# Fourier filter and routed experts on one core: the sign copy goes to VectorE, some transfers are cut anew, and the written-out order is planned again

## The chip, the cores and the metric

One core of one Trainium2 chip. The metric is the device time in microseconds (us) of one execution, as a median over runs. TensorE (PE, with its weight loads PEld), VectorE (DVE), ScalarE (ACT), GpSimd (POOL) and the transfers that SyncE (SP) and POOL issue all run side by side; every engine takes its own instructions in the order in which the kernel wrote them.

## The reference

```
X  = rfft(x, axis=1)                      # x: 8 x 2496 x 256, float32
Yr = X.real @ w_r - X.imag @ w_i + b_r
Yi = X.real @ w_i + X.imag @ w_r + b_i
Y  = soft_threshold(Yr, 0.01) + 1j * soft_threshold(Yi, 0.01)
t  = irfft(Y, n=2496, axis=1).reshape(19968, 256)
e  = argmax(t @ w_gate);  g = softmax(t @ w_gate)[e]       # 8 experts
out = g * (relu(t @ w1[e]) @ w2[e])       # w1: 256 x 1024, w2: 1024 x 256 per expert
```

## The kernel before

**Forward part.** The transform of length 2496 = 39 x 64 is two steps of matmuls. For each of 8 batches: x is loaded in six pieces (`load_x`), `s1` does the step of 39 in fp32, its result goes out to DRAM (`s1_store`, tile zd) and comes back turned (`zload`, tile zs) in five pieces of four frequencies. Each piece i then runs through a chain: `s2` (step of 64, fp32, with the constant cd), `s2_hi` on ACT and `s2_lo` on DVE split the result into two f16 halves in tile xa, `s2_neg` writes the negative of one third of xa into another third (line 542, on POOL), `wmul` multiplies by the complex weight (48 matmuls, lines 554 to 556, the last 24 of which read the negated part), `thr`, `thr_pos`, `thr_sub`, `thr_out`, `thr_lo` are the threshold and a second split (DVE, ACT, DVE, ACT, POOL line 586), `inv1` (lines 600 and 602, constant ce; line 602 reads what `thr_lo` wrote) is the first step back, and `vstore` puts it to DRAM (vd).

**Back part.** For each batch `vload`, `inv2`, a split, a transpose, the logits, the routing on DVE, and 22 scatters by POOL (line 770) that put token rows into the list of their expert. Batches 0 and 1 go back early, the others during the expert phase. `vzero` writes zeros behind each batch's part of vd, `fillers` writes 256 rows of no token ahead of each expert's list, from a tile that takes the only buffer "cl", which `thr_pos` needs for every piece.

**Expert weights.** 16 matrices are loaded (`wprep_load`), measured, split into f16 halves (ACT, and DVE line 818) and stored. The first expert block waits for the tables of batches 0 and 1 and for all 16.

**Expert part.** 92 blocks (71 of 256 rows, 21 of 128): `fetch_x`, `fetch_w`, `up` (lines 983 to 985), relu and split (lines 989, 994, 999), `down` (lines 1010 to 1012), a gate on ACT and a scatter to the output by POOL (line 1021).

**Order.** `Plan` places all this. Every piece of work is a task with an engine, a cost, predecessors, buffers and a rank; when an engine is idle the plan takes the ready task of lowest rank whose buffers are free. A transfer of rank above 0 is held while the planned transfer backlog exceeds BACK; one of rank 0 or less is not held. ORDER adds to the rank by kind of task, MARGIN adds a delay after the last predecessor, BEGIN replaces a task's earliest time, INV0 and INVD set when batches from 2 on may go back, WT0 and WTD when the matrices may be loaded (matrix u from WT0 + WTD x u). The plan only writes the order of instructions on each engine; on the chip each waits for its semaphores.

```
ld = A("SP", 1.0, wprep_load, u, take=[wa], dma=3.25, rank=0.5, after=WT0 + WTD * u)
n_ = A("POOL", 1.6, s2_neg, b, i, deps=[l], rank=0, early=1.5)
if t["dma"] and t["rank"] > 0 and dq - now > BACK:
```

Of the kernel before, what the change touches and what calls it, by code (L numbers as in the profile page):

```python
# [22 lines left out]
SLOTS = 22  # L23
K1 = 20
# [104 lines left out]
BUF = {"bt": 2, "zt": 2, "zs": 2, "xa": 2, "u": 2, "cl": 1, "sh": 1, "vt": 2, "vs": 2, "yt": 2, "yr": 6}  # L129
EPOCHS = {2:12,3:22,4:31,5:41,6:51,7:61}  # L130
JS, NPRE = 12, 2
SCD = 2.6
INV0, INVD, WT0, WTD = 355, 85, 135, 9
ORDER = {"fetch_x": -19, "inv1": 37, "inv1_hi": -7, "inv1_lo": -22, "inv2:p": -261, "inv2_hi:p": -3, "inv2_lo:p": -42,
    "load_x": 53, "load_x:0": 42, "logits:p": -73, "norm_part": 60, "route3:p": 44, "route_hot:p": 45,
    "s1": -48, "s1_store": 22, "s2_lo": -39, "s2_neg": -60, "scatter:p": -3, "table": 29, "thr_lo": -26,
    "thr_pos": 29, "thr_sq": 17, "vstore": 12, "w_lo": -14, "wmul": 70, "wprep_hi": 27, "wprep_lo": 27,
    "wprep_scale": 16, "wprep_sq": 30, "wprep_store": 33, "xscale": 9, "ynorm:p": 148, "yscale:l": 40,
    "ytrans:p": 45}
MARGIN = {"inv2:l": 3, "inv2:p": 5, "logits:l": 1, "logits:p": 11, "norm_sum": 6, "route2:l": 0, "route2:p": 7,  # L140
    "s2": 2, "wprep_sum": 3, "ynorm:l": 5}
BEGIN = {"fillers": 81, "load_b": 15, "load_cd": 28, "load_ce": 47, "load_g": 23, "load_rest": 70, "load_w": 5,
    "vzero": 52}
ZD = 3
KS = 4

# [21 lines left out]
class Plan:  # L168


    LAT, DLAT, BACK = 0.2, 2.0, 3

    def __init__(self, bufs):
        self.t, self.bufs, self.mark = [], bufs, {}
# [101 lines left out]
def build(ctx: ExitStack, tc: tile.TileContext, x, w_r, w_i, b_r, b_i, wg, w1, w2,  # L276
          c_c, c_cg, c_d, c_e, c_tri, c_32, c_blk, out):
    nc = tc.nc
    B = x.shape[0]
    V, S, P, T, Q = nc.vector, nc.scalar, nc.gpsimd, nc.tensor, nc.sync  # L280
# [4 lines left out]
    dram = ctx.enter_context(tc.tile_pool(name="dram", bufs=1, space=bass.MemoryType.DRAM))  # L285
# [17 lines left out]
    fpool = fw.enter_context(tc.tile_pool(name="fp", bufs=2))  # L303
# [25 lines left out]
    cd = fcst.tile([128, K1, 128], F32, name="cd")  # L329
    ce = fcst.tile([128, K1, 2, 128], F16, name="ce")  # L330
# [13 lines left out]
        for q in range(4):  # L344
            Q.dma_start(wgs[32 * q:32 * q + 32], wg.rearrange("(b i o) e -> i b o e", i=32, o=2))

    def load_cd():
        Q.dma_start(cd, c_d.rearrange("p (k m) -> p k m", k=K1))

    def load_ce():  # L350
        Q.dma_start(ce, c_e.rearrange("p (k h m) -> p k h m", k=K1, h=2))

    def load_rest():
        Q.dma_start(c32, c_32)
# [7 lines left out]
    zero = fpool.tile([128, 1024], F16, name="vt", bufs=BUF["vt"])  # L362
    V.memset(zero, 0.0)

    zd = [dram.tile([K1, 66, 2, D], F32, name=f"zd{i}") for i in range(ZD)]
    vd = [dram.tile([K1, 66, 2, 512], F16, name=f"vd{i}") for i in range(B)]

    def vzero():
        for i in range(B):
            Q.dma_start(vd[i][:, 64:66].rearrange("k n r c -> k n (r c)"), bc(zero[:K1, :], 2))  # L370


    sc = cst.tile([128, 16], F32, name="sc")
# [165 lines left out]
    def s2_neg(b, i):  # L539
        xa = st[b][("xa", i)]  # L540
        xf = xa.rearrange("p j h c -> p (j h) c")
        P.tensor_scalar(xf[:, :, 0:64], xf[:, :, 128:192], -1.0, None, op0=ALU.mult)  # L542

    def wmul(b, i):

# [278 lines left out]

    def fillers():

        fr = fpool.tile([128, RC], F16, name="cl", bufs=BUF["cl"])
        V.memset(fr, 0.0)
        V.memset(fr[:, 512:514].bitcast(I32), 1 << 24)
        fu = fr.bitcast(U16)  # L830
        rv = rows.rearrange("(e r) c -> e r c", e=NE)
        for e in range(NE):
            Q.dma_start(rv[e, 0:256, 0:RC].rearrange("(h p) c -> p h c", p=128), bc(fu, 2))


    MX = max(n for _, _, n, _ in TABS)
# [182 lines left out]
    def down_store(j, t):  # L1019
# [3 lines left out]
        for k in scat2:  # L1023
# [25 lines left out]
    def ns_(c):  # L1049
        return min(4, SLOTS - 4 * c)  # L1050


    wu, zv, fcl = L.buf("u"), L.buf("vt"), L.buf("cl")
    i_cc = A("SP", 0.5, load_cc, rank=0, dma=0.2)
    ld0 = [A("SP", 1.3, load_x, 0, 4 * c, min(SLOTS, 4 * c + 4), rank=0, dma=2.3 * ns_(c) / 4) for c in range(6)]
    i_w = A("SP", 1.6, load_w, rank=0, dma=1.8, take=[wu])
    i_b = A("SP", 1.2, load_b, rank=0, dma=0.6)
    i_g = A("SP", 1.7, load_g, rank=0, dma=0.5)
    i_cd = A("SP", 0.8, load_cd, rank=0, dma=4.8)
    i_r = A("SP", 1.8, load_rest, rank=0.4, dma=2.0, after=26.0)  # L1060
    i_ce = A("SP", 0.8, load_ce, rank=0.2, dma=4.5, after=25.0)
    i_z = A("SP", 4.0, vzero, rank=0.4, dma=0.5, after=40.0, free=[zv])
    A("PE", 6.9, warm, 16, rank=0, take=[zv], free=[zv])
    p_q = A("ACT", 2.0, wsquare, deps=[i_w, i_b, i_g], rank=1)
    p_s = A("PE", 0.2, wsum, deps=[p_q], rank=-100)
# [3 lines left out]
    wp_ = A("DVE", 1.6, w_lo, deps=[wh_], rank=0.5, free=[wu])  # L1069
    gp_ = A("ACT", 0.8, g_hi, deps=[p_p], rank=0.6)  # L1070
    gp_ = A("DVE", 0.8, g_lo, deps=[gp_], rank=0.6)
    fl = A("SP", 5.0, fillers, rank=5, dma=4.0, after=60.0, take=[fcl], free=[fcl])
    s1l, nps, lastz = {}, {}, {}
    scat_t, rt3, tabs, prevtab = {}, {}, {}, None
    last_tab = {}
# [5 lines left out]
    for u in range(2 * NE):  # L1081
        wa, wb = L.buf(f"wt{u % 2}0"), L.buf(f"wt{u % 2}1")
        ld = A("SP", 1.0, wprep_load, u, take=[wa], dma=3.25, rank=0.5, after=WT0 + WTD * u)
        sq = A("ACT", 2.1, wprep_sq, u, deps=[ld], rank=1.2)
        sm_ = A("PE", 0.2, wprep_sum, u, deps=[sq, wst_.get(("sc", u - 1))], rank=-100)
        scl = wst_["sc", u] = A("DVE", 1.5, wprep_scale, u, deps=[sm_], rank=1, take=[wb])
        for i in range(2):
            h = A("ACT", 0.95, wprep_hi, u, i, deps=[scl], rank=1.2)
            l = A("DVE", 1.2, wprep_lo, u, i, deps=[h], rank=1.2, free=[wa])
            wst_[u, i] = A("SP", 0.5, wprep_store, u, i, deps=[l], dma=1.4, rank=0.5, free=[wb])  # L1090
    wdone = [t for k, t in wst_.items() if k[0] != "sc"]

# [1 line left out]
    for b in range(B):  # L1094
        F = 10 * b

        ld = [] if b else ld0
        for c in range(6):
            if b:
                ld.append(A("SP", 1.3, load_x, b, 4 * c, 4 * c + ns_(c), deps=[s1l[b - 1, c], nps[b - 1][c]],  # L1100
                            rank=0.3, dma=9.2 * ns_(c) / 22))
        nm = A("DVE", 0.1, norm, b, deps=[fin1.get(("xs", b - 1))])
        nps[b] = [A("DVE" if not b and i % 2 else "ACT", 1.05, norm_part, b, i, deps=[nm, ld[i]], rank=1)
# [16 lines left out]
        for i in range(5):  # L1120
            zs_, p2_, xa_, pw_, u_, cl_, sh_, pa_, vt_ = (L.buf(n) for n in ("zs", "mm", "xa", "mm", "u", "cl", "sh", "mm", "vt"))
            zl = A("SP", 0.55, zload, b, i, deps=sts, take=[zs_], free=[zdb], dma=8.8 / 5, rank=0)
            t = A("PE", 1.82, s2, b, i, deps=[zl, i_cd], take=[p2_, xa_], free=[zs_], rank=F + 3)
            h = A("ACT", 1.0, s2_hi, b, i, deps=[t, xs], rank=1)
            l = A("DVE", 1.2, s2_lo, b, i, deps=[h], free=[p2_], rank=1)
            n_ = A("POOL", 1.6, s2_neg, b, i, deps=[l], rank=0, early=1.5)
            w = A("PE", 5.22, wmul, b, i, deps=[n_, wp_], take=[pw_, u_], free=[xa_], rank=F + 2)
            th = A("DVE", 1.15, thr, b, i, deps=[w, xs], free=[pw_, btb], rank=0)
            cl = A("ACT", 1.05, thr_pos, b, i, deps=[th], take=[cl_], rank=0)
            sb_ = A("DVE", 1.21, thr_sub, b, i, deps=[cl], free=[cl_], rank=0)  # L1130
            hi = A("ACT", 0.96, thr_out, b, i, deps=[sb_], take=[sh_], free=[u_], rank=0)
            lo = A("POOL", 2.15, thr_lo, b, i, deps=[hi], free=[u_], rank=0, early=0.8)
            sqs.append(A("ACT", 1.05, thr_sq, b, i, deps=[sb_], free=[u_], rank=0.5))
            v1 = A("PE", 1.32, inv1, b, i, deps=[lo, hi, i_ce], take=[pa_, vt_], free=[sh_], rank=F + 1)
            h = A("ACT", 0.92, inv1_hi, b, i, deps=[v1], rank=0)
            l = A("DVE", 1.15, inv1_lo, b, i, deps=[h], free=[pa_], rank=0)
            vst.append(A("SP", 0.6, vstore, b, i, deps=[l], free=[vt_], dma=8.8 / 5, rank=0))
# [9 lines left out]
        for c in range(6):  # L1147
            k = ns_(c) / 4
# [46 lines left out]
    for j in range(NB):  # L1195
# [3 lines left out]
                       take=[xb_[j], tb_[j]], dma=1.95 if j < NF else 0.98, rank=1.2 + j * 1e-3, prev=ft.get(j - 1))  # L1199
# [47 lines left out]
```

## Time and profile before

| | |
|---|---|
| median of 3 runs | 1435.89 us (1434.1 to 1438.23) |
| the profiled execution: time | 1442.84 us |
| its span, first to last instruction | 1441.0 us |
| mean granted TensorE clock | 0.985 |
| PE busy | 1384.8 us |
| DVE / ACT / POOL busy | 877.3 / 661.9 / 578.2 us |
| transfers | 330.01 MB, mean 229 GB/s |

Busy time and waits are those of the profiled execution; 1.84 us of its time lie outside the span. The granted clock is a share of full speed, so that 0.5 is the lower of TensorE's two levels. The share of the 16 transfer engines can read a little over 1 in a short stretch.

### The profile page before, as it was taken

Reading aid. Unit: us, or ns where it says so; the run is one execution under the profiler, and the core shown is the slowest. Engines: PE = TensorE matmul, PEld = TensorE weight load, DVE = VectorE, ACT = ScalarE, POOL = GpSimd, SP = SyncE. Lnnn points to the kernel's source line nnn. Section 1 sums busy time; section 2 is a strip of 40 time slices with the busy share of each in tenths; the row PEclk is TensorE's granted clock in tenths of the full one; section 3 lists DMA queues with packets and bytes.
Section 4 is the critical chain, followed back from the end, with each engine's and each line's share of the span. In section 5 each row is a group of like instructions: output and inputs, shape, how many; then the busy total and the mean of one; then the engine's idle time right before and its main releaser. Section 6 shows DMA issues by size and latency. Waiting matters only on the chain.

```text
span 1441.0 us, 33479 instructions
## 1 busy us (share of the span) xinstructions
PE 1384.8 (96%) x12842; PEld 1181.3 (82%) x12842; DVE 877.3 (61%) x1736; ACT 661.9 (46%) x869; POOL 578.2 (40%) x471
## 2 busy tenths in 40 slices
PE   5889999999998899999999999999999999999998
PEld 2667778767887688888888888888888888889997
DVE  2335777988898897557567566557467543343443
ACT  4557799788895452332333333333332222222222
POOL 0334345586457723533443434433423531111211
PEclk8899999999999999999999999999999999999999
DMA  8898999989996657668897977987774484658873
GB/s 247 241 273 249 302 307 308 312 264 321 315 313 200 221 136 195 182 150 266 232 269 207 291 214 228 255 224 216 211 255 126 124 265 114 193 138 282 210 185 117
DMA packets 260337, 330.01 MB, mean 229 GB/s; under 512 B 124758, under 2 KB 219512, under 8 KB 245329
## 3 DMA queue, kind: packets, MB, share of 16 engines
q1 hardware_dynamic: 243904, 286.78, 68.4%
q0 software_dynamic: 16272, 41.09, 8.1%
q8 instruction: 101, 1.65, 0.5%
q14 instruction: 60, 0.48, 0.1%
HBM read 276.61 MB, written 106.76 MB: 266 GB/s over the span
## 4 chain that ended last, share of the span: by engine, by line
PE 80%; DVE 5%; DMA 5%; issue 5%; POOL 4%; ACT 2%; SPq 1%; POOLq 0%; ACTq 0%; DVEq 0%
PE mm L983 10%; PE mm L984 10%; PE mm L985 10%; PE pob L1010 10%; PE pob L1011 10%; PE pob L1012 10%; PE mm L652 3%; PE mm L497 3%; PE mm L554 3%; PE mm L556 3%; PE mm L555 3%; PE mm L526 3%; POOL rows L770 2%; DMA x<-x 1%; PE mm L600 1%
## 5 line engine op out<-in xcount | busy, mean ns | idle before, releaser
L1021 POOL DMA_INDIRECT out<-o,ix x163 | 167.7, 1029 | 546.2 <-ACT o L1017 468.3
L984 PE MATMUL mm<-xt,wt 128*128 128x256 f16 (+1 forms) x1472 | 366.9, 260 | 0.2 <-issue 0.2
L983 PE MATMUL mm<-xt,wt 128*128 128x256 f16 (+1 forms) x1472 | 367.0, 260 | 0.0
L985 PE MATMUL mm<-xt,wt 128*128 128x256 f16 (+1 forms) x1472 | 366.9, 260 | 0.0
L1010 PE MATMUL pob<-wt,hh 128*128 128x256 f16 x1304 | 355.5, 273 | 0.9 <-ACT o L1017 0.6
L1012 PE MATMUL pob<-wt,hh 128*128 128x256 f16 x1304 | 355.4, 273 | 0.5 <-issue 0.4
L1011 PE MATMUL pob<-wt,hh 128*128 128x256 f16 x1304 | 355.4, 273 | 0.3 <-issue 0.2
L989 ACT ACTIVATE r<-mm 128x1024 f32<-128x1024 f32 x163 | 166.8, 1023 | 366.9 <-PE mm L985 271.0
L994 DVE CAST hh<-r 128x1024 f16<-128x1024 f32 x163 | 114.9, 705 | 294.3 <-ACT r L989 279.0
L770 POOL DMA_INDIRECT rows<-yr,ix x176 | 188.2, 1069 | 59.5 <-issue 52.2
L999 DVE TENSOR_TENSOR hh<-r,hh 128x1024 f16<-128x1024 f32 x163 | 199.8, 1225 | 5.6
L1017 ACT ACTIVATE o<-pob,g 128x256 f32<-128x256 f32 x163 | 76.0, 473 | 249.2 <-PE pob L1012 246.0
L554 PE MATMUL mm<-w,xa 128*128 128x256 f16 x640 | 176.0, 275 | 7.1 <-DVE u L563 2.6
L542 POOL TENSOR_SCALAR xa<-xa 128x1024 f16<-128x1024 f16 x40 | 114.1, 2854 | 168.6 <-DVE xa L536 143.6
L555 PE MATMUL mm<-w,xa 128*128 128x256 f16 x640 | 175.9, 275 | 0.0
L556 PE MATMUL mm<-w,xa 128*128 128x256 f16 x640 | 175.8, 275 | 0.0
L984 PEld LDWEIGHTS <-wt 128*128 128x128 f16 x1472 | 144.0, 98 | 15.7 <-issue 0.5
L983 PEld LDWEIGHTS <-wt 128*128 128x128 f16 x1472 | 144.0, 98 | 15.4
L985 PEld LDWEIGHTS <-wt 128*128 128x128 f16 x1472 | 143.9, 98 | 12.9
L1010 PEld LDWEIGHTS <-hh 128*128 128x128 f16 x1304 | 127.5, 98 | 16.7 <-issue 1.4
L1011 PEld LDWEIGHTS <-hh 128*128 128x128 f16 x1304 | 127.6, 98 | 16.4 <-issue 1.1
L1012 PEld LDWEIGHTS <-hh 128*128 128x128 f16 x1304 | 127.5, 98 | 15.9 <-issue 1.1
(169 smaller groups left out, 1964.4 us busy)
## 6 DMA issues: line engine op xcount, KB each, us to landing
wt<-wsc SPq DMA_DIRECT2D x184, 1024.0 KB
zs<-zd SPq DMA_DIRECT2D x40, 512.0 KB
vd<-vt SPq DMA_DIRECT2D x40, 512.0 KB
vs<-vd SPq DMA_DIRECT2D x80, 240.0 KB
x<-x SPq DMA_DIRECT2D x120, 156.0 KB
zd<-zt SPq DMA_DIRECT2D x74, 240.0 KB
wt<-moe_w SPq DMA_DIRECT2D x32, 512.0 KB
wsc<-wt SPq DMA_DIRECT2D x32, 512.0 KB
```

What stands on the lines that cost most here:

```text
L554: T.matmul(o, lh, w16[:, r, h, 0, :], start=(h == 0 and r == 0 and k % 2 == 0), stop=False)
L555: T.matmul(o, lh, w16[:, r, h, 1, :], start=False, stop=False)
L556: T.matmul(o, ll, w16[:, r, h, 0, :], start=False, stop=(h == 1 and r == 1 and k % 2 == 1))
L770: i = P.indirect_dma_start(out=rows, out_offset=bass.IndirectOffsetOnAxis(ap=s["ix"][:, j:j + 1], axis=0), in_=s[("yr", j // 4)][:, j % 4, ...
L983: T.matmul(pv[:, a, :], wh, xt[:, h, :], start=(h == 0), stop=False)
L984: T.matmul(pv[:, a, :], wh, xt[:, 2 + h, :], start=False, stop=False)
L985: T.matmul(pv[:, a, :], wl, xt[:, h, :], start=False, stop=(h == 1))
L999: V.tensor_tensor(hh[:, :, 1, :], H.pop(("r", j, q)).rearrange("p (a n) -> p a n", n=n), hh[:, :, 0, :], ALU.subtract)
L1010: T.matmul(po, hi, wh, start=(fc == 0), stop=False)
L1011: T.matmul(po, hi, wl, start=False, stop=False)
L1012: T.matmul(po, lo, wh, start=False, stop=(fc == 7))
L1021: i = P.indirect_dma_start(out=out, out_offset=bass.IndirectOffsetOnAxis(ap=ix[:, t:t + 1], axis=0), in_=H.pop(("o", j, t)), in_offset=Non ...
```

## The change

`s2_neg` moves from POOL to DVE. The zeros behind vd become two transfers of 80 rows in place of eight of 20. The rows of no token are written two per run of the tile. The constants cd and ce are loaded in five pieces each, and each piece of `s2` and `inv1` waits for its own piece alone. Costs in the plan are set anew, BACK falls from 3 to 2.5, and ORDER, MARGIN, BEGIN, INV0, INVD, WT0 and WTD are new; `load_cd`, `load_w` and `load_g` have no BEGIN any more, batch 0's `load_x` no addition to its rank, and `wprep_load` gets -50, so that its rank goes from 0.5 to -49.5.

```
-INV0, INVD, WT0, WTD = 355, 85, 135, 9
-ORDER = {"fetch_x": -19, "inv1": 37, "inv1_hi": -7, "inv1_lo": -22, "inv2:p": -261, "inv2_hi:p": -3, "inv2_lo:p": -42,
-    "load_x": 53, "load_x:0": 42, "logits:p": -73, "norm_part": 60, "route3:p": 44, "route_hot:p": 45,
-    "s1": -48, "s1_store": 22, "s2_lo": -39, "s2_neg": -60, "scatter:p": -3, "table": 29, "thr_lo": -26,
-    "thr_pos": 29, "thr_sq": 17, "vstore": 12, "w_lo": -14, "wmul": 70, "wprep_hi": 27, "wprep_lo": 27,
-    "wprep_scale": 16, "wprep_sq": 30, "wprep_store": 33, "xscale": 9, "ynorm:p": 148, "yscale:l": 40,
-    "ytrans:p": 45}
-BEGIN = {"fillers": 81, "load_b": 15, "load_cd": 28, "load_ce": 47, "load_g": 23, "load_rest": 70, "load_w": 5,
-    "vzero": 52}
+INV0, INVD, WT0, WTD = 375, 118, 97, 11
+ORDER = {"down_store": -3, "inv1": 142, "inv1_lo": 5, "inv2:p": -131, "inv2_lo:l": 22, "load_ce": 27, "load_rest": 19,
+    "load_x": 84, "logits:l": -8, "norm": 12, "norm_part": 71, "route1:p": 14, "route_hot:p": 40,
+    "s1_store": 17, "s2": 84, "s2_hi": -27, "scatter:p": -22, "table": 29, "thr_lo": -75, "thr_out": 1,
+    "thr_pos": 20, "thr_sq": 14, "thr_sub": 8, "vload:p": -12, "wmul": 198, "wparts": -27, "wprep_hi": 31,
+    "wprep_lo": 26, "wprep_load": -50, "wprep_scale": 21, "wprep_store": 25, "wprep_sum": -127,
+    "ynorm:p": 225, "yscale:l": 69, "ytrans:l": 14, "ytrans:p": 51}
+BEGIN = {"fillers": 77, "load_b": 18, "load_ce": 48, "load_rest": 95, "vzero": 35}
...
-    def load_cd():
-        Q.dma_start(cd, c_d.rearrange("p (k m) -> p k m", k=K1))
+    def load_cd(i):
+        Q.dma_start(cd[:, 4 * i:4 * i + 4, :], c_d.rearrange("p (k m) -> p k m", k=K1)[:, 4 * i:4 * i + 4, :])
...
-        for i in range(B):
-            Q.dma_start(vd[i][:, 64:66].rearrange("k n r c -> k n (r c)"), bc(zero[:K1, :], 2))
+        for i in range(0, B * K1, 80):
+            Q.dma_start(vall[i:i + 80, 64:66].rearrange("k n r c -> k n (r c)"), bc(zero[:80, :], 2))
...
-        P.tensor_scalar(xf[:, :, 0:64], xf[:, :, 128:192], -1.0, None, op0=ALU.mult)
+        V.tensor_scalar(xf[:, :, 0:64], xf[:, :, 128:192], -1.0, None, op0=ALU.mult)
...
-            Q.dma_start(rv[e, 0:256, 0:RC].rearrange("(h p) c -> p h c", p=128), bc(fu, 2))
+            Q.dma_start(rv[e, 0:256, 0:RC].rearrange("(p h) c -> p h c", h=2), fu)
...
-    i_cd = A("SP", 0.8, load_cd, rank=0, dma=4.8)
+    i_cd = [A("SP", 0.45, load_cd, i, rank=0, dma=1.0) for i in range(5)]
...
-            n_ = A("POOL", 1.6, s2_neg, b, i, deps=[l], rank=0, early=1.5)
+            n_ = A("DVE", 0.75, s2_neg, b, i, deps=[l], rank=0, early=0.7)
```

## Rows read from the trace of the kernel before

**Rows 1.** The page, part 1: busy time of each engine
```profile
PE 1384.8 (96%) x12842; PEld 1181.3 (82%) x12842; DVE 877.3 (61%) x1736; ACT 661.9 (46%) x869; POOL 578.2 (40%) x471
```
**Rows 2.** Stretches of 20 us: busy by engine, granted clock, transfer share, GB/s
```profile
core 0: us, PE busy (x) PEld busy (x) DVE busy (x) ACT busy (x) POOL busy (x), PEclk, DMA share, GB/s
...
20.00:40.00 20.00, 2.67 (x7) 1.50 (x7) 6.75 (x37) 7.39 (x17) 0.00 (x0) 0.54 0.90 275
...
100.00:120.00 20.00, 15.77 (x91) 10.88 (x90) 10.10 (x20) 13.97 (x19) 6.99 (x3) 0.83 0.97 297
...
140.00:160.00 20.00, 19.65 (x141) 14.63 (x140) 11.82 (x10) 12.40 (x15) 8.96 (x7) 1.00 1.06 297
...
300.00:320.00 20.00, 16.66 (x121) 12.68 (x120) 16.17 (x12) 17.10 (x23) 17.59 (x13) 0.91 0.76 228
...
460.00:480.00 20.00, 14.79 (x132) 13.08 (x131) 17.30 (x27) 9.43 (x11) 18.51 (x11) 1.00 0.47 149
480.00:500.00 20.00, 16.01 (x128) 13.10 (x128) 16.54 (x30) 8.38 (x10) 17.56 (x13) 0.83 0.79 295
...
1200.00:1220.00 20.00, 20.00 (x185) 17.93 (x184) 8.13 (x11) 5.99 (x8) 3.04 (x4) 1.00 0.56 159
```
**Rows 3.** Waits of PE: line, releaser: us in total, times, longest
```profile
PE mm L602 <- POOL sh L586: 10.6, 8, 2.7
PE mm L526 <- DMA zs<-zd: 10.5, 2, 9.4
PE sm L402 <- ACT junk L395: 6.4, 1, 6.4
PE mm L497 <- DVE u L563: 4.3, 2, 4.1
PE mm L497 <- DMA x<-x: 3.3, 2, 3.0
PE mm L554 <- DVE u L563: 2.6, 1, 2.6
...
PE mm L554 <- POOL xa L542: 2.1, 1, 2.1
```
**Rows 4.** Timeline of SP's queue, 0 to 120 us
```profile
27.33 0.85 SPq L511 DMA_DIRECT2D zd<-vs  x2
...
29.51 0.36 SPq L348 DMA_DIRECT2D cd<-c_d  x1
...
51.38 9.01 SPq L370 DMA_DIRECT2D vd<-vt  x8
...
86.95 6.76 SPq L833 DMA_DIRECT2D rows<-cl  x8
```
**Rows 5.** Chain of waits in order of time: the start
```profile
29.97 9.90 DMA zs<-zd
```
**Rows 6.** Chain of waits in order of time: 80 to 130 us
```profile
86.95 7.18 DMA rows<-cl
94.20 9.85 DMA vd<-vt
104.08 1.16 ACT cl L569
```
**Rows 7.** Timelines of POOL and of DVE around 486 us
```profile
484.81 2.82 POOL L542 TENSOR_SCALAR xa<-xa 128x1024 f16<-128x1024 f16 x1
487.56 2.15 POOL L586 TENSOR_TENSOR sh<-u,sh 128x1024 f16<-128x1024 f32 x1
...
485.96 3.79 DVE L920 TENSOR_SCALAR tab<-t_False 128x12 int32<-128x12 int32 x1
```
**Rows 8.** Single lines: ns of one, least/median/most, first and last start
```profile
L542 POOL TENSOR_SCALAR xa<-xa x40: 2762/2768/3737, 46.3 to 494.9; 128x1024 f16<-128x1024 f16 x40
...
L994 DVE CAST hh<-r x163: 628/694/1710, 517.1 to 1431.3; 128x1024 f16<-128x1024 f32 x163
...
L536 DVE SCALAR_TENSOR_TENSOR xa<-mm,sb,xa x40: 1242/1284/1285, 44.9 to 493.5; 128x1024 f16<-128x1024 f32 x40
...
L575 DVE SCALAR_TENSOR_TENSOR u<-u,sb,cl x40: 1185/1278/3181, 57.7 to 513.6; 128x1024 f32<-128x1024 f32 x40
...
L818 DVE SCALAR_TENSOR_TENSOR wt<-wt,wn,wt x32: 1272/1278/3155, 170.0 to 445.7; 128x1024 f16<-128x1024 f32 x32
```
**Rows 9.** Groups by line: transfer-free price of a plain DVE write
```profile
L363 DVE MEMSET vt<- 128x512 uint32 x1 | 0.5, 485 | 0.1
```
**Rows 10.** The page, part 6: the matrices' transfers
```profile
wt<-moe_w SPq DMA_DIRECT2D x32, 512.0 KB
```

More of the change, by code (lines that the diff above doesn't have):

```diff
@@ L132 @@
 SCD = 2.6
-INV0, INVD, WT0, WTD = 355, 85, 135, 9
-ORDER = {"fetch_x": -19, "inv1": 37, "inv1_hi": -7, "inv1_lo": -22, "inv2:p": -261, "inv2_hi:p": -3, "inv2_lo:p": -42,
-    "load_x": 53, "load_x:0": 42, "logits:p": -73, "norm_part": 60, "route3:p": 44, "route_hot:p": 45,
-    "s1": -48, "s1_store": 22, "s2_lo": -39, "s2_neg": -60, "scatter:p": -3, "table": 29, "thr_lo": -26,
-    "thr_pos": 29, "thr_sq": 17, "vstore": 12, "w_lo": -14, "wmul": 70, "wprep_hi": 27, "wprep_lo": 27,
-    "wprep_scale": 16, "wprep_sq": 30, "wprep_store": 33, "xscale": 9, "ynorm:p": 148, "yscale:l": 40,
-    "ytrans:p": 45}
-MARGIN = {"inv2:l": 3, "inv2:p": 5, "logits:l": 1, "logits:p": 11, "norm_sum": 6, "route2:l": 0, "route2:p": 7,
-    "s2": 2, "wprep_sum": 3, "ynorm:l": 5}
-BEGIN = {"fillers": 81, "load_b": 15, "load_cd": 28, "load_ce": 47, "load_g": 23, "load_rest": 70, "load_w": 5,
-    "vzero": 52}
+INV0, INVD, WT0, WTD = 375, 118, 97, 11
[5 more added lines that the diff above has]
+    "ynorm:p": 225, "yscale:l": 69, "ytrans:l": 14, "ytrans:p": 51}
+MARGIN = {"inv2:l": 10, "inv2:p": 7, "logits:l": 1, "logits:p": 8, "norm_sum": 3, "route2:l": 0, "route2:p": 4,
+    "s2": 2, "wmul": 1, "wprep_sum": 4.5, "ynorm:l": 13, "ynorm:p": 18}
+BEGIN = {"fillers": 77, "load_b": 18, "load_ce": 48, "load_rest": 95, "vzero": 35}
 ZD = 3
@@ L168 @@
 class Plan:
-    LAT, DLAT, BACK = 0.2, 2.0, 3
+    LAT, DLAT, BACK = 0.2, 2.0, 2.5
     def __init__(self, bufs):
@@ L345, in load_g, with load_ce @@
             Q.dma_start(wgs[32 * q:32 * q + 32], wg.rearrange("(b i o) e -> i b o e", i=32, o=2))
-    def load_cd():
-        Q.dma_start(cd, c_d.rearrange("p (k m) -> p k m", k=K1))
-    def load_ce():
-        Q.dma_start(ce, c_e.rearrange("p (k h m) -> p k h m", k=K1, h=2))
+    def load_cd(i):
+        Q.dma_start(cd[:, 4 * i:4 * i + 4, :], c_d.rearrange("p (k m) -> p k m", k=K1)[:, 4 * i:4 * i + 4, :])
+    def load_ce(i):
+        Q.dma_start(ce[:, 4 * i:4 * i + 4], c_e.rearrange("p (k h m) -> p k h m", k=K1, h=2)[:, 4 * i:4 * i + 4])
     def load_rest():
@@ L365, in build @@
     zd = [dram.tile([K1, 66, 2, D], F32, name=f"zd{i}") for i in range(ZD)]
-    vd = [dram.tile([K1, 66, 2, 512], F16, name=f"vd{i}") for i in range(B)]
+    vall = dram.tile([B * K1, 66, 2, 512], F16, name="vd")
+    vd = [vall[i * K1:(i + 1) * K1] for i in range(B)]
     def vzero():
-        for i in range(B):
-            Q.dma_start(vd[i][:, 64:66].rearrange("k n r c -> k n (r c)"), bc(zero[:K1, :], 2))
+        for i in range(0, B * K1, 80):
+            Q.dma_start(vall[i:i + 80, 64:66].rearrange("k n r c -> k n (r c)"), bc(zero[:80, :], 2))
     sc = cst.tile([128, 16], F32, name="sc")
@@ L825, in fillers @@
     def fillers():
-        fr = fpool.tile([128, RC], F16, name="cl", bufs=BUF["cl"])
+        fr = fpool.tile([128, 2, RC], F16, name="cl", bufs=BUF["cl"])
         V.memset(fr, 0.0)
-        V.memset(fr[:, 512:514].bitcast(I32), 1 << 24)
+        V.memset(fr[:, :, 512:514].bitcast(I32), 1 << 24)
         fu = fr.bitcast(U16)
@@ L1054, in build @@
     i_cc = A("SP", 0.5, load_cc, rank=0, dma=0.2)
-    ld0 = [A("SP", 1.3, load_x, 0, 4 * c, min(SLOTS, 4 * c + 4), rank=0, dma=2.3 * ns_(c) / 4) for c in range(6)]
+    ld0 = [A("SP", 1.5, load_x, 0, 4 * c, min(SLOTS, 4 * c + 4), rank=0, dma=2.3 * ns_(c) / 4) for c in range(6)]
     i_w = A("SP", 1.6, load_w, rank=0, dma=1.8, take=[wu])
@@ L1058, in build @@
     i_g = A("SP", 1.7, load_g, rank=0, dma=0.5)
-    i_cd = A("SP", 0.8, load_cd, rank=0, dma=4.8)
+    i_cd = [A("SP", 0.45, load_cd, i, rank=0, dma=1.0) for i in range(5)]
     i_r = A("SP", 1.8, load_rest, rank=0.4, dma=2.0, after=26.0)
-    i_ce = A("SP", 0.8, load_ce, rank=0.2, dma=4.5, after=25.0)
-    i_z = A("SP", 4.0, vzero, rank=0.4, dma=0.5, after=40.0, free=[zv])
+    i_ce = [A("SP", 0.45, load_ce, i, rank=0.2, dma=1.0, after=25.0) for i in range(5)]
+    i_z = A("SP", 2.0, vzero, rank=0.4, dma=1.5, after=40.0, free=[zv])
     A("PE", 6.9, warm, 16, rank=0, take=[zv], free=[zv])
@@ L1071, in build @@
     gp_ = A("DVE", 0.8, g_lo, deps=[gp_], rank=0.6)
-    fl = A("SP", 5.0, fillers, rank=5, dma=4.0, after=60.0, take=[fcl], free=[fcl])
+    fl = A("SP", 5.5, fillers, rank=5, dma=6.0, after=60.0, take=[fcl], free=[fcl])
     s1l, nps, lastz = {}, {}, {}
@@ L1087, in build @@
         for i in range(2):
-            h = A("ACT", 0.95, wprep_hi, u, i, deps=[scl], rank=1.2)
-            l = A("DVE", 1.2, wprep_lo, u, i, deps=[h], rank=1.2, free=[wa])
+            h = A("ACT", 1.04, wprep_hi, u, i, deps=[scl], rank=1.2)
+            l = A("DVE", 1.36, wprep_lo, u, i, deps=[h], rank=1.2, free=[wa])
             wst_[u, i] = A("SP", 0.5, wprep_store, u, i, deps=[l], dma=1.4, rank=0.5, free=[wb])
@@ L1099, in build @@
             if b:
-                ld.append(A("SP", 1.3, load_x, b, 4 * c, 4 * c + ns_(c), deps=[s1l[b - 1, c], nps[b - 1][c]],
+                ld.append(A("SP", 1.5, load_x, b, 4 * c, 4 * c + ns_(c), deps=[s1l[b - 1, c], nps[b - 1][c]],
                             rank=0.3, dma=9.2 * ns_(c) / 22))
@@ L1122, in build @@
             zl = A("SP", 0.55, zload, b, i, deps=sts, take=[zs_], free=[zdb], dma=8.8 / 5, rank=0)
-            t = A("PE", 1.82, s2, b, i, deps=[zl, i_cd], take=[p2_, xa_], free=[zs_], rank=F + 3)
+            t = A("PE", 1.82, s2, b, i, deps=[zl, i_cd[i]], take=[p2_, xa_], free=[zs_], rank=F + 3)
             h = A("ACT", 1.0, s2_hi, b, i, deps=[t, xs], rank=1)
             l = A("DVE", 1.2, s2_lo, b, i, deps=[h], free=[p2_], rank=1)
-            n_ = A("POOL", 1.6, s2_neg, b, i, deps=[l], rank=0, early=1.5)
+            n_ = A("DVE", 0.75, s2_neg, b, i, deps=[l], rank=0, early=0.7)
             w = A("PE", 5.22, wmul, b, i, deps=[n_, wp_], take=[pw_, u_], free=[xa_], rank=F + 2)
@@ L1129, in build @@
             cl = A("ACT", 1.05, thr_pos, b, i, deps=[th], take=[cl_], rank=0)
-            sb_ = A("DVE", 1.21, thr_sub, b, i, deps=[cl], free=[cl_], rank=0)
+            sb_ = A("DVE", 1.26, thr_sub, b, i, deps=[cl], free=[cl_], rank=0)
             hi = A("ACT", 0.96, thr_out, b, i, deps=[sb_], take=[sh_], free=[u_], rank=0)
@@ L1133, in build @@
             sqs.append(A("ACT", 1.05, thr_sq, b, i, deps=[sb_], free=[u_], rank=0.5))
-            v1 = A("PE", 1.32, inv1, b, i, deps=[lo, hi, i_ce], take=[pa_, vt_], free=[sh_], rank=F + 1)
+            v1 = A("PE", 1.32, inv1, b, i, deps=[lo, hi, i_ce[i]], take=[pa_, vt_], free=[sh_], rank=F + 1)
             h = A("ACT", 0.92, inv1_hi, b, i, deps=[v1], rank=0)
```

## Prediction

> **What bounds the kernel now.** I read the page's first part, then the stretches of 20 us, then PE's waits, then the chain of waits where PE stands. PE is busy for 1384.8 of 1441.0 us [rows 1], so that all idle time of the engine that bounds the kernel is 56 us, and nothing in the change takes a matmul away. The stretches say where the 56 us lie [rows 2]. From 500 us on PE is full at full clock (20.00 of 20 in 1200 to 1220): whatever the new plan moves there, the late batches above all, costs and gains next to nothing as long as PE stays fed. The loss is in the first 500 us and has three places. The start: 17.3 us idle in 20 to 40. The stretch 100 to 120: 4.2 us idle and a clock of 0.83. The stretches 300 to 320 and 460 to 500: 3.3, 5.2 and 4.0 us idle, clock 0.91 and 0.83 in the first and the last. A clock of 0.83 over 20 us is 6.8 us at the lower level, which loses 3.4 us of full-speed work; 0.91 loses 1.8. The waits name the causes [rows 3]: 9.4 us for the first zs, 4.1 us for a product buffer that DVE's `thr` had not emptied, 10.6 us in eight waits for `thr_lo` on POOL, 2.1 us for the sign copy on POOL.
>
> **The sign copy on DVE: POOL's side.** POOL gives up 40 x 2.77 = 111 us [rows 8]. POOL is at 17.6 to 18.5 of 20 us where the scatters of batches 0 and 1 run [rows 2], and there the copy of 2.8 us stands in POOL's order with `thr_lo`. No wait for `thr_lo` is longer than 2.7 us [rows 3], less than one copy. At most all of 10.6 + 2.1 = 12.7 us goes, with 5.2 us of clock behind it, together 18; at least nothing, if the scatters (which stay) are what holds `thr_lo`, and no loss on POOL is possible, as it only gives work away. I take 8 of the 12.7 (a scatter ahead of `thr_lo` still costs its own time) and 2 of the 5.2: **-10**.
>
> **DVE's side.** No row shows an f16 to f16 copy of 1024 columns on DVE. The nearest are the cast from f32 of the same size, 628 ns at the least, and the writing of as many bytes, 485 ns [rows 8, 9]; from above the two-operand split `s2_lo`, 1284 ns. I take 630 ns, as the cast is the same kind of one-operand work: 40 x 0.63 = 25 us (19 to 51) on an engine that has 17.3 and 16.5 of 20 in its tightest stretches, 460 to 500. Some comes back: a DVE instruction on 12 columns took 3.79 us at 485.96 and ended when POOL's two had ended (487.56 + 2.15 = 489.71) [rows 7], and lines 575 and 818 run to 3181 and 3155 ns where their median is 1278 [rows 8]. So POOL's long instructions hold DVE up, and 40 of the 80 long ones go. But the copy now stands in DVE's order between `s2_lo` and `thr`, and both `thr` and the next `s2_lo` wait behind it, with `wmul` and the product buffer behind those. In 460 to 500 some four pieces pass: 4 x 0.63 = 2.5 us of 6.2 idle DVE us, so PE sees little. Price **+3**, from 0 (DVE's gain from POOL pays for it) to +10 (the copy shows in full in the 16 or so pieces between 280 and 320 and from 400 on).
>
> The Trainium skill (SBUF — State Buffer, section SBUF: two separate sides) says that GpSimd and VectorE share one pair of ports as an exclusive lock, which a VectorE instruction in a two-port mode also needs. The trace agrees as far as the row at 485.96 goes. By that rule the new copy could itself stand behind a `thr_lo`; that is a rival below.
>
> **Start.** The constant cd goes out at 29.51, right ahead of the first zs at 29.97, which takes 9.90 us to land [rows 4, 5]. With cd loaded before the stores of zd, those 1280 KB are out of the way of zs: at 275 GB/s [rows 2] 4.8 us. But the same bytes now stand ahead of the zd stores, and the queue was at 0.90 of its engines; it mostly changes who waits. What can be won is the order: the last zd store of batch 0 went out only at 27.33 [rows 4], behind other loads. I take **-3**, from -9 (the whole wait for zs) to +5 (cd shows in full ahead of the stores).
>
> **Fillers and cl.** From 86.95 the eight filler transfers and the v store behind them keep `thr_pos` waiting until 104.08 [rows 6], and PE stands for the 4.1 us named above, at a loss of 3.4 us of clock. Runs of two rows halve the count of runs, and the new plan counts the transfer as longer, so it should hide the wait better. The buffer is still held for over ten us. **-3**, from -8 (both go) to +4 (a longer wait at another place).
>
> **Zeros, pieces of ce, SP's order.** `vzero` holds SP for 9.01 us from 51.38 [rows 4]; with two transfers in place of eight some 6.8 us of SP are saved. PE has no wait there, and all that time is covered by ready matmuls: 0. Without that cover (vzero is earlier now, at a planned 35, with PE idle) it would cost SP two issues, 2.3 us. The pieces add 4 issues per constant; the cd issue took 0.36 us, so 1.4 us of SP each, ahead of the zd stores for cd: inside the bounds of the start.
>
> **Matrices.** `wprep_load` now goes ahead of everything, from a planned 97 in place of 135, and is not held by the backlog. They are 32 x 512 KB [rows 10], 16.8 MB, 56 us at 297 GB/s, put into stretches whose transfer share is 0.97 and 1.06 already [rows 2]. In the trace the split of the matrices ran from 170.0 to 445.7 [rows 8], and buffers limit how far it can run ahead. Price **+2**, from 0 to half of the 56 us.
>
> **Sum.** -10 + 3 - 3 - 3 + 2 = -11. Against the profiled execution's own 1442.84 that is 1431.8; the median of the runs lies 6.95 below it, at 1435.89, and the forecast for it is **1425**.
>
> **Rivals.** (a) Slower: the matrices' loads starve the forward part. Place: 100 to 300 us, the x loads and zs behind 1 MB of matrix each time. With the other terms kept (-13), half of the 56 us showing gives +15: 1451. It decides from 17 us on that PE waits for x or zs in these stretches. For it: a transfer share of 0.97 to 1.06; against it: in the whole span PE waited 3.3 us for x and, past the first, 1.1 us for zs [rows 3], and the split on ACT and DVE paces the loads. 0.2. (b) DVE takes POOL's place: the gain of 10 goes, because the scatters hold `thr_lo` anyway, or the copy stands on DVE behind `thr_lo`'s 2.15 us or behind the tables. Without the gain the sum is 3 - 3 - 3 + 2 = -1; with it and DVE's price at its upper end, -10 + 10 - 3 - 3 + 2 = -4: 1432 to 1435. For it: DVE at 17.3 of 20; against it: DVE loses POOL's long holds. This also is the case that the sign copy was not what PE waited for. 0.2. (c) All three places close: -18 + 3 - 9 - 8 + 2 = -30: 1406. For it: every wait listed is of a kind that another order removes; against it: a first zs cannot come before its data have crossed DRAM twice. 0.1.
>
> **How the numbers follow.** The forecast has 0.5, (a) 0.2, (b) 0.2, (c) 0.1. The forecast's own range, from its bounds, is 1412 to 1434; the range for 8 in 10 reaches into (c) to 1408 and into (a) to 1445. A measurement can tell some 0.3%, 4.3 us, from no change, that is 1431.6 to 1440.2. Faster: the forecast without its upper end (0.45), (c) (0.1) and a little of (b) (0.05) make 0.60. Same: the most of (b) and the forecast's end, 0.18. Slower: (a) and a mishap with no name, 0.22.
>
> **What would show it.** Right: POOL busy some 111 us less, no wait of `inv1` for `thr_lo` over 1 us, line 575's longest instruction under 2.5 us; the first zs landing before 38; PE idle in 460 to 500 under 4 us in place of 9.2; the DVE copy at 0.5 to 0.8 us. Wrong: PE waits for x or zs between 100 and 300 (a); new waits of `wmul` for the DVE copy, or `thr_lo` as late as before behind scatters (b); PE idle after 500 us, which I hold at nothing, if a late batch's rows come too late.

## The result and the profile after

The changed kernel takes 1422.29 us (median of 4 runs, 1418.31 to 1423.08) against 1436.12 for the kernel before in the same comparison: a ratio of **0.9898** (95% interval 0.9874 to 0.9922), 13.8 us less where 11 were forecast. A later comparison gave 0.9945 (0.9925 to 0.9966), there against a median of 1444.86. Both intervals lie wholly below 1, so the kernel is faster, by half to one per cent; the first gain is larger than the forecast's 0.75% and the second smaller. Ratios below belong to the comparison in which they were taken; the later one of the changed kernel (e0) is on the same chip as e1 to e5, e9 and e10.

The profiled execution took 1421.71 us, near its median, where that of before had been 6.95 above its own. So the two spans (1441.0 and 1419.9) differ by 21, which is more than the change is worth.

The page's first part and header, which answer to [rows 1]:

```profile
span 1419.9 us, 33476 instructions
...
PE 1377.1 (97%) x12842; PEld 1178.5 (83%) x12842; DVE 897.5 (63%) x1776; ACT 660.7 (47%) x869; POOL 456.0 (32%) x431
```

POOL lost 122 us and DVE gained 20. PE is busy 7.7 us less with the same 12842 matmuls, which fits a mean granted clock of 0.991 in place of 0.985; its idle time fell from 56.2 to 42.8.

The same stretches of 20 us as in [rows 2], and the two in which the scatters of batch 1 now run (420 to 460):

```profile
20.00:40.00 20.00, 5.96 (x10) 2.73 (x10) 6.12 (x35) 7.39 (x17) 0.00 (x0) 0.57 0.92 268
...
100.00:120.00 20.00, 17.98 (x140) 14.54 (x140) 11.40 (x23) 17.74 (x26) 4.90 (x3) 1.00 0.88 286
...
300.00:320.00 20.00, 18.61 (x119) 13.28 (x119) 18.66 (x23) 13.99 (x16) 16.27 (x17) 0.91 0.95 298
...
420.00:440.00 20.00, 18.46 (x165) 16.20 (x163) 18.50 (x39) 11.31 (x16) 16.02 (x13) 1.00 0.74 241
440.00:460.00 20.00, 18.08 (x159) 15.91 (x157) 17.25 (x24) 12.27 (x15) 16.51 (x15) 1.00 0.72 216
460.00:480.00 20.00, 20.00 (x197) 18.34 (x195) 15.82 (x37) 10.07 (x12) 4.82 (x2) 1.00 0.78 251
480.00:500.00 20.00, 17.92 (x161) 13.82 (x159) 15.20 (x29) 11.12 (x13) 4.93 (x5) 0.91 0.55 149
```

The stretch 100 to 120 has its full clock, and 460 to 500 is idle for 2.1 us in place of 9.2; where the scatters now run, 420 to 460, 3.5 us are lost (1.7 before). Over 420 to 500 together PE's idle time fell from 10.9 to 5.5 us. PE's waits, which answer to [rows 3]:

```profile
PE mm L497 <- DMA x<-x: 10.1, 1, 10.1
PE sm L402 <- ACT junk L395: 5.7, 1, 5.7
PE mm L602 <- POOL sh L586: 4.6, 4, 1.5
PE mm L554 <- DVE xa L536: 3.5, 4, 1.6
PE mm L600 <- DVE u L563: 3.3, 2, 1.9
...
PE mm L526 <- DMA zs<-zd: 0.9, 2, 0.6
```

The waits for `thr_lo` fell from 10.6 to 4.6 us. The 9.4 us for the first zs are gone by name only: PE now waits 10.1 us for batch 1's x. PE's timeline shows it:

```profile
34.63 5.66 PE L497 MATMUL mm<-x,cc 117*128 117x512 f32 x8 [10.11 <-DMA x<-x]
40.50 3.81 PE L526 MATMUL mm<-cd,zs 128*128 128x128 f32 x32 [0.22 <-DMA zs<-zd]
```

The first `s2` starts at 40.50 (39.97 before, where the zs transfer of [rows 5] ended). What was won at the start is that two pieces of batch 1's `s1` stand ahead of it.

Two more lines, of single instructions: the copy, and the first `up` of the first expert block, which tells how long the forward part and the routing of batches 0 and 1 took. It started at 512.8 before:

```profile
L542 DVE TENSOR_SCALAR xa<-xa x40: 417/427/2264, 45.0 to 475.7; 128x1024 f16<-128x1024 f16 x40
...
L983 PE MATMUL mm<-xt,wt x1472: 219/272/283, 495.2 to 1408.7; 128*128 128x256 f16 x142, 128*128 128x128 f16 x42
```

17.6 of the 21 us between the two profiles are there by the first expert block.

Seven of the 40 copies took over 1 us. The longest, with what ran on POOL:

```profile
196.75 2.13 POOL L586 TENSOR_TENSOR sh<-u,sh 128x1024 f16<-128x1024 f32 x1 [11.52 <-ACT sh L581]
...
196.90 2.26 DVE L542 TENSOR_SCALAR xa<-xa 128x1024 f16<-128x1024 f16 x1
```

It began 0.15 us after a `thr_lo` and ended 0.28 us after that one's end. All seven are of this kind: each began 0.15 to 1.33 us into a `thr_lo` and ended 0.28 to 0.29 us after it. The copies that began together with a `thr_lo`, or before it, took their 0.43 us.

### The profile page after: what moved, and what is told of

The parts are those of the page before. It is cut to its first block, busy times and chain, and to the rows that moved or that the text cites. A ratio compares the mean times of both kernels' runs of the same rounds, so it can differ in the third digit from the quotient of the medians.

```text
span 1419.9 us, 33476 instructions
## 1 busy us (share of the span) xinstructions
PE 1377.1 (97%) x12842; PEld 1178.5 (83%) x12842; DVE 897.5 (63%) x1776; ACT 660.7 (47%) x869; POOL 456.0 (32%) x431
## 4 chain that ended last, share of the span: by engine, by line
PE 76%; DMA 8%; DVE 6%; issue 4%; ACT 4%; POOL 1%; SPq 1%; POOLq 0%; ACTq 0%; DVEq 0%
PE mm L983 10%; PE mm L984 10%; PE mm L985 10%; PE pob L1010 10%; PE pob L1011 10%; PE pob L1012 10%; PE mm L652 3%; PE mm L554 2%; PE mm L556 2%; PE mm L555 2%; PE mm L526 2%; DMA x<-x 2%; PE mm L497 2%; DMA vd<-vt 1%; DMA zs<-zd 1%
## 5 line engine op out<-in xcount | busy, mean ns | idle before, releaser
L989 ACT ACTIVATE r<-mm 128x1024 f32<-128x1024 f32 x163 | 167.0, 1024 | 347.7 <-PE mm L985 283.3
L586 POOL TENSOR_TENSOR sh<-u,sh 128x1024 f16<-128x1024 f32 x40 | 86.8, 2170 | 351.8 <-ACT sh L581 351.7
```

Of the source, the lines that this page charges most:

```text
L989: S.activation(r, H.pop((j, q, 0)), AF.Relu, scale=2.0 ** -15)
```

## The experiments

The theory after the result, before these runs: the copy is worth what the prediction said (7 us), the transfers a little, the order the rest. Rivals: the order alone does it; or the parts overlap. All kernels were timed in 5 rounds beside the kernel before. "First block" is the first start of the expert part in each kernel's profile, once each.

| run | what differs | ratio to before (95%) | first block |
|---|---|---|---|
| before | | 1 | 512.8 |
| e1 | before + copy on DVE | 0.9957 (0.9941 to 0.9973) | 505.3 |
| e2 | changed, copy on POOL | 0.9982 (0.9968 to 0.9996) | 510.2 |
| e3 | before + transfers | 0.9925 (0.9907 to 0.9942) | 499.7 |
| e4 | changed, old transfers | 0.9961 (0.9948 to 0.9975) | 506.8 |
| e0 | changed, again | 0.9945 (0.9925 to 0.9966) | 500.9 |
| e5 | new order alone | 1.0006 (0.9993 to 1.0019) | 510.7 |
| e9 | before + copy + transfers | 0.9918 (0.9901 to 0.9934) | 498.8 |
| e10 | before + fillers | 0.9978 (0.9964 to 0.9993) | 509.8 |
| e13 | before + zeros | 0.9972 (0.9957 to 0.9987) | 502.1 |
| e8 | before, fillers off cl | 0.9986 (0.9971 to 1.0000) | 508.5 |
| e14 | e9, fillers off cl | 0.9907 (0.9886 to 0.9927) | 494.8 |
| e6 | changed, copy made twice | 0.9990 (0.9974 to 1.0006) | 504.2 |

e13, e8, e14 and e6 ran beside each other on another chip than the rest of the table.

**e1, the copy alone.**

```
-        P.tensor_scalar(xf[:, :, 0:64], xf[:, :, 128:192], -1.0, None, op0=ALU.mult)
+        V.tensor_scalar(xf[:, :, 0:64], xf[:, :, 128:192], -1.0, None, op0=ALU.mult)
```

> The kernel before with the sign copy on DVE and nothing else; the order of every engine is kept, so the copy stands in DVE's order where the plan had placed it on POOL. Theory (the copy is worth some 7 to 10 us through POOL's queue, in 440 to 520 above all): 1426 to 1430 against some 1436, the waits of inv1 for thr_lo (10.6 us before) down to 5 or less, 440 to 520 some 5 us shorter in idle. Rival b (the scatters hold thr_lo, DVE takes POOL's place): within 4 us of before, thr_lo waits still 8 or more, or new waits of wmul for the DVE copy. The copy itself on DVE: 0.42 us where POOL is idle, up to 2.3 where it is not, as in the changed kernel.

0.9957 is 6.2 us. Waits of PE in e1:

```profile
PE mm L554 <- DVE u L563: 3.6, 3, 2.6
PE mm L602 <- POOL sh L586: 3.6, 2, 2.0
...
PE mm L554 <- DVE xa L536: 2.7, 3, 1.1
```

POOL's part went as the theory had it, 10.6 to 3.6, and the wait for the copy on POOL (2.1) is gone. Over 440 to 520 PE's idle time fell from 10.9 to 5.3 us, also as expected. DVE took a part of it: 3.6 and 2.7 where 2.6 and 1.4 had been, and 17.2 where 14.0 had been if all of PE's waits for DVE up to 520 us are added up.

**e2, the copy undone.** The line above, the other way round, in the changed kernel.

> The changed kernel with the copy back on POOL, every engine's order otherwise kept. Theory (the copy is worth 7 to 10 us): 1429 to 1432, with POOL at 570 us busy and the waits of inv1 for thr_lo back at 8 us or more. Rival (the new order alone makes the gain): 1420 to 1425, as the changed kernel. A third case: since the new order counts on a copy that is done 0.75 us after the split, losing that could cost more than the copy is worth in the old order: 1435 or more.

0.9982 against the 0.9945 of e0 on the same chip: 0.37 points, 5 us, with intervals that just do not touch. It is about the size of e1, in another order. The waits for `thr_lo` rise beyond those of before, which fits an order that was planned for a free POOL but is not shown to come from it:

```profile
PE mm L602 <- POOL sh L586: 14.5, 6, 5.6
```

**e3, the transfers alone.** The old order, with the diff's new `vzero`, `fillers` and constants; a constant's five pieces go out one after the other where it stood:

```
     def load_cd():
-        Q.dma_start(cd, c_d.rearrange("p (k m) -> p k m", k=K1))
+        for i in range(5):
+            Q.dma_start(cd[:, 4 * i:4 * i + 4, :], c_d.rearrange("p (k m) -> p k m", k=K1)[:, 4 * i:4 * i + 4, :])
```

> The kernel before with the new transfers (zeros in two, rows of no token two per run, constants in five pieces each, issued one after the other at the old places) and the old order and copy. Theory (transfers alone are worth little, as PE has no wait at the zeros and the cl wait stands): 1432 to 1437, the wait of thr_pos on the fillers still there. Rival (the longer runs shorten the hold on cl): 1428 to 1431, thr_pos freed by 100 us in place of 104, PE's wait of 4.1 us gone.

0.9925, 11 us: the largest of all parts, and more than the rival expected. Its stretches of 20 us:

```profile
80.00:100.00 20.00, 20.00 (x151) 15.88 (x149) 10.22 (x12) 12.62 (x16) 9.78 (x4) 1.00 0.99 320
100.00:120.00 20.00, 19.88 (x154) 15.91 (x153) 11.86 (x32) 18.61 (x28) 8.72 (x4) 1.00 0.95 290
```

PE is full where it had been idle for 5.4 us (1.2 in 80 to 100, 4.2 in 100 to 120), and the clock of 0.83 in 100 to 120 [rows 2] is 1.00. And `thr_pos` runs at 93.98, not at 104.08 [rows 6].

**e4, the transfers undone.** In the changed kernel, `vzero` and `fillers` as before, and each constant whole in its first piece's place.

> The changed kernel with the old transfers at the new places (each constant whole where its first piece stood, zeros in eight, one row per run). Theory (worth little): 1421 to 1426. Rival (the new order needs the pieces or the short zeros, which now stand at 35 us where PE is idle): 1427 or more, with PE's first s2 later by 2 us or more than in the changed kernel, where it starts at 40.5.

0.9961 against 0.9945: the intervals overlap, so what the transfers are worth in the new order is not settled by this; it looks like less than in the old one. The rival's sign did not come: PE's first `s2` starts at 39.98.

**e5, the order alone.** e2 and e4 together, and **e9**, the counterpart: e1 and e3 together, the old order. **e0** is the changed kernel itself beside them.

> The changed kernel once more, beside the next three, so that all of them stand against the same chip: 0.987 to 0.992 of before.

> The changed kernel with both the copy and the transfers undone, every engine's order kept: the new order by itself. Undoing the copy cost 0.8% of the gain and undoing the transfers 0.6%, so theory A (the parts add, the order by itself is worth nothing or a little less than nothing) says 1.000 to 1.006 of before. Theory B (the order holds part of what each of the two gives, so that both overlap with it) says 0.994 to 0.999.

> The kernel before with the copy on DVE and the new transfers, in the old order. They gave 0.9957 and 0.9925 one at a time. Theory A (they add, and the order is worth nothing): 0.987 to 0.990, as the changed kernel. Theory B (they overlap, since a wait that one takes away leaves slack that the other would have used, and the new order is what gathers both): 0.991 to 0.994.

e0 came out above what was expected of it (0.9945). The order alone is worth nothing that shows: 1.0006 (0.9993 to 1.0019). Neither theory A nor B has it whole: A is right on the order, but e1 and e3 seem not to add in full (0.9957 x 0.9925 = 0.988, e9 has 0.9918), as B said. e9 and e0, on the same chip, cannot be told apart. So no run here shows a gain from the new ranks; that the first comparison's 0.9898 holds some is left open, as e9 was not timed there. The order does move time at the start (PE is idle 18.1 us up to 40 us in e5, 21.7 before), but none of it is left at the end. e5's waits are

```profile
PE mm L603 <- POOL sh L587: 14.2, 6, 5.7
PE mm L498 <- DMA x<-x: 10.3, 1, 10.3
```

the first of them 3.6 us longer than before.

**e10, the fillers alone**, the diff's two lines in `fillers`.

> The kernel before with the rows of no token two per run and nothing else. Theory (the gain of the transfers is the shorter hold on cl): 0.992 to 0.995, cl free some 11 us after the filler tile is written in place of 18, no wait of PE between 100 and 120 and full clock there. Rival (the gain comes from the short zeros or the pieces, or from the first 60 us): 0.998 to 1.001, cl held as long as before.

0.9978, 3 us: the time is close to the rival's, while `cl` did come free sooner. `thr_pos` starts at 99.35, some 14 us after the tile is written, in place of 18. The stretches show that the fillers are not the whole of e3:

```profile
80.00:100.00 20.00, 17.84 (x136) 14.15 (x136) 6.63 (x7) 10.69 (x15) 7.63 (x3) 1.00 0.95 293
100.00:120.00 20.00, 16.92 (x105) 12.40 (x104) 11.96 (x21) 15.97 (x22) 7.00 (x3) 0.91 0.90 269
```

Against [rows 2] PE is busy 1.15 us more in 100 to 120, of the 4.23 that it had lost there, and the clock is 0.91 in place of 0.83; 80 to 100 is short too.

**e13, the zeros alone.**

```
-        for i in range(B):
-            Q.dma_start(vd[i][:, 64:66].rearrange("k n r c -> k n (r c)"), bc(zero[:K1, :], 2))
+        for i in range(0, B * K1, 80):
+            Q.dma_start(vall[i:i + 80, 64:66].rearrange("k n r c -> k n (r c)"), bc(zero[:80, :], 2))
```

> The kernel before with the zeros behind v in two transfers of 80 rows in place of eight of 20, and nothing else. The prediction held this to be worth nothing, as PE has no wait while SP issues the eight. The new transfers together gave 0.9925, the fillers alone 0.9978. Theory C (the 9 us of SP are handed on along SP's own order to the zd stores, zs and x loads behind them, and come out at the next place where PE is short, 85 to 112): 0.993 to 0.997, with the stores after the zeros some 6 us earlier. Theory D (nothing, as predicted; then the pieces of the constants or the pairing with the fillers carry the 0.5%): 0.998 to 1.001.

0.9972, 4 us (2 to 6), for an edit that the prediction held at nothing; the value lies between the two theories, nearer to C. The edit also makes the eight DRAM tiles of vd slices of one, and what that does by itself was not run. SP's queue in e13, to be read beside [rows 4]:

```profile
50.34 1.54 SPq L371 DMA_DIRECT2D vd<-vt  x2
51.98 1.69 SPq L512 DMA_DIRECT2D zd<-zt  x2
57.50 0.38 SPq L516 DMA_DIRECT2D zs<-zd  x1
...
59.75 6.72 SPq L319 DMA_DIRECT2D x<-x  x9
...
83.41 6.20 SPq L834 DMA_DIRECT2D rows<-cl  x8
```

The same places in the kernel before, and two of SP's waits there:

```profile
60.48 0.80 SPq L511 DMA_DIRECT2D zd<-zt  x2
61.38 0.76 SPq L515 DMA_DIRECT2D zs<-zd  x1
...
63.80 7.64 SPq L319 DMA_DIRECT2D x<-x  x9
```

```profile
SPq L370 <- DMA ce<-c_e: 4.1, 1, 4.1
...
SPq L370 <- DMA zs<-zd: 1.1, 1, 1.1
```

The store behind the zeros goes out at 51.98; in the kernel before it stood until 60.48, behind the eight. Of these 8.5 us, 3.9 are left at the next zs, 4.1 at the next loads of x and 3.5 at the fillers; e13's queue had been 1.0 us ahead before the zeros already. The waits say what the 9.01 us of the eight zeros were: the issues themselves took 0.27 to 0.88 us each, 3.5 us together, and for 5.2 us SP stood ahead of the seventh and the eighth, until a load of ce and one of zs had landed. PE's stretches, first before, then in e13:

```profile
80.00:100.00 20.00, 18.84 (x149) 15.26 (x149) 6.90 (x8) 10.86 (x14) 7.64 (x3) 1.00 0.97 263
```

```profile
80.00:100.00 20.00, 20.00 (x151) 15.90 (x149) 7.66 (x9) 9.48 (x12) 7.64 (x3) 1.00 1.06 279
100.00:120.00 20.00, 17.71 (x130) 13.67 (x129) 13.16 (x35) 19.78 (x29) 9.73 (x4) 1.00 0.95 300
```

80 to 120 is idle for 2.3 us in place of 5.4, and its clock is full in place of 0.83 in the second half.

**e8, the fillers off cl.**

```
-        fr = fpool.tile([128, RC], F16, name="cl", bufs=BUF["cl"])
+        fr = pool.tile([128, 4, RC], F16, name="yr", bufs=BUF["yr"])[:, 0, :]
```

> The kernel before with the filler rows written from a buffer of the tile yr, which is free until 140 us, so that thr_pos does not wait for the transfers; order and transfers as before. It prices the hold on cl by itself. Theory (the hold is what PE pays for at 100 to 112): 0.993 to 0.996, no wait of thr_pos there, full clock in 100 to 120. Rival (the transfers' time in the queue is what delays, whoever holds the tile): 0.998 to 1.001, PE short in the same stretch for x or zs.

0.9986, with an interval that reaches 1: the rival is nearer. `thr_pos` no longer waits, but PE is as short as before in 100 to 120, and the waits of ACT and PE in 90 to 125 name the stores of zd:

```profile
100.00:120.00 20.00, 15.64 (x112) 11.99 (x111) 8.74 (x18) 13.88 (x19) 4.90 (x2) 1.00 0.97 301
```

```profile
ACT zt L504 <- DMA zd<-zt: 5.0, 2, 4.3
...
PE mm L600 <- ACT zt L504: 3.5, 2, 2.7
```

The chain of waits has the fillers' transfer at 90.64 for 11.33 us. So with the hold gone the same transfers stopped the kernel in another way: the stores of zd stood behind them, and `s1_out` behind those stores.

**e14, a try for a better version**: e9 with the filler rows in yr.

> A try for a version that beats both: the old order with the copy on DVE, the new transfers, and the filler rows off cl. The old order with copy and transfers gave 0.9918, the changed kernel 0.9945 on this chip. If the hold on cl still costs after the fillers were made shorter: 0.988 to 0.991. If the shorter fillers already took that away (PE has no wait left in 80 to 130): 0.991 to 0.993.

0.9907, with a first block at 494.8, as early as the changed kernel's best. The interval overlaps with e9's and with both comparisons of the changed kernel, so this is no proven improvement; no difference to the changed kernel shows, and it has none of the new ranks.

**e6, the copy made twice.** The line of e1 stands twice in the changed kernel; the values are the same.

> The changed kernel with every sign copy on DVE made twice (the same values written again), so that the cost of DVE's time is doubled: 40 x 0.42 to 0.66 us more. Theory (DVE has slack enough, as the prediction's term of +3, from 0 to +10, says): 0.995 to 0.998, at most 4 us over the changed kernel's 0.9945. Rival b (DVE has taken POOL's place as what PE waits for): 0.999 or more, with PE's waits for xa and u up by 6 us or more.

0.9990 against 0.9945, on another chip, with intervals that do not touch. But two comparisons of the changed kernel itself, 0.9898 and 0.9945, lie 0.47 points apart, so these 0.45 points cannot be put down to the second copy. DVE is busy 20.7 us more than in e0 (902.99 against 882.30 up to 1400). PE's longest waits for DVE are these:

```profile
PE mm L555 <- DVE xa L536: 3.8, 4, 2.1
...
PE mm L555 <- DVE u L564: 2.2, 2, 1.3
```

The one for xa had been 2.7 in e0. The rise is well under the 6 us that rival b wanted to see. All of PE's waits for DVE up to 520 us add up to 17.3 us against 12.6 in e0: doubling the copy does cost PE something, while the ratio leaves open how much of it reaches the end.

## Why the prediction was right, and where it was not

**The sum** was right in size: -11 forecast, -13.8 and about -8 measured. That was in part luck. The copy came as forecast, -6.2 for -7. The transfers were worth 11 us (e3) where the fillers' 3 stood for all of them, and the start and the matrices, -1 together, nothing that shows (e5). The parts add up to 17; what brought the sum back is that copy and transfers together gave only 11.8 (e9), and no term stood for that overlap.

**The signs.** POOL is busy 122 us less and line 575's longest instruction fell from 3181 to 1308 ns, as asked. The longest wait for `thr_lo` is 1.5 us, where none over 1 was to be left, and the first zs did not land before 38.

**The copy, -10 and +3: right in their sum.** e1 gives -6.2 us, the undoing in e2 5 us. POOL's waits went from 12.7 to 4.6, that is 8.1 less; I had taken 8. One copy was to take 0.63 us: it takes 0.43 where nothing is in its way, and 0.66 in the mean (26.5 us for 40), because seven of them took up to 2264 ns behind a `thr_lo`. So 25 us forecast, 26.5 measured, from another mixture: the instruction is faster than the cast, and the hold that was a rival there takes the difference. The Trainium skill's rule of the exclusive lock (SBUF — State Buffer, section SBUF: two separate sides) fits: every copy that began well inside a `thr_lo` ended 0.28 to 0.29 us after it. DVE's hold-ups by POOL did not all go: line 575 has a mean of 1280 (1343 before), but line 818 rose from 1445 to 1545.

**DVE as the next bound, rival (b): did not come.** The copy did gain (e1, e2). But DVE's time is not free either, where I had all but hidden it in slack: PE's waits for DVE up to 520 us rose by 3.2 us in e1, as the +3 had it, and by 4.7 when the copy was made twice (e6 against e0, one profile each). What that costs at the end is open.

**The start, -3: seen at its place, for another reason, and not at the end.** PE is idle 3.7 us less up to 40 us (21.7 and 18.1). The first zs did not land earlier, as I had wanted to see (before 38); the order put other work ahead of `s2`. e5 has the same gain at the start and is no faster than before.

**The fillers, -3: right in size.** 0.9978, 3 us. Whether my mechanism, the hold on cl, is what paid is open: e8, which takes the hold away and leaves the transfers, shows 2 us with an interval from 0 to 4, and PE as short in 100 to 120 as before.

**The zeros, 0: wrong.** The step read: PE has no wait there, and all that time is covered by ready matmuls. The cover was real at that place, and the delay was not spent there: SP issues in order, so what the eight cost was handed on to the stores and loads behind them (in e13 the first goes out 8.5 us earlier, the fillers 3.5), until PE ran short at 85 to 112. e13: 4 us. The place where SP stood and the place where PE paid lay some 30 us and more apart. The price of 2.3 us for two issues was misread too: most of the 9.01 us was SP's wait for two landings, and the two new transfers took 0.93 us in the changed kernel.

**The pieces**, which I had put inside the start's bounds, were not run by themselves. What e3 has beyond fillers and zeros (0.9978 x 0.9972 = 0.9950 against 0.9925) is theirs or that of the pairing, or only noise: 0.9950 lies 0.0008 outside e3's interval and has an uncertainty of its own.

**The matrices, +2: nothing that shows.** Rival (a) did not come. The first split of a matrix moved from 170.0 to 132.5 and the last from 445.7 to 425.6, and in 100 to 300 us PE waits for no x and no zs at all.

**After 500 us: nothing, as forecast.** PE is busy for all 880.00 us between 520 and 1400 in the changed kernel's first profile (877.67 before). In e0 it was 875.70; 3.5 of the 4.3 us idle there name no releaser but issue.

**The ranks, not costed by themselves:** I had spread them over the terms. Nothing measurable came of them alone (e5), and nothing that could be told apart on top of the parts (e9 against e0, one chip).

## What to carry to other kernels

A queue that issues in order carries a delay along: price a blocking burst of transfers where the transfers behind it are next needed, not where it stands. When a change bundles parts and a new order, run the order alone and the parts alone; here a few edits to transfers and the move of one instruction made the gain, and the new ranks none that shows. Moving work off a busy side engine pays for what it frees in that engine's order; look for what comes back as waits for the engine that takes it (3.2 us more of PE's in e1), even where that engine has idle time.

## What was not expected of the hardware

Eight transfers of 20 partitions held SP for 9.01 us, though their issues took only 3.5: it stood 4.1 and 1.1 us until earlier transfers had landed. Two of 80 took 1.54 (e13). A VectorE copy of 1024 f16 columns took 417 to 427 ns (least and median) where GpSimd took 2762 to 2768; and when it began well inside a `thr_lo` on GpSimd, it ended 0.28 to 0.29 us after that one. And comparisons differ: the kernel before has medians of 1436.12, 1445.28, 1444.86 and 1440.57 us in the four, and the changed kernel's ratio was 0.9898 in one and 0.9945 in another, further apart than the interval of either allows; why is open.
